# Both attention products that close a quad moved into one slot, the small one into the first projection's banks

## The chip, the core and the metric

The kernel runs on one core of one Trainium2 chip. A core has a matrix engine (TensorE, PE in the profile, with its weight loads shown apart as PEld), VectorE (DVE), ScalarE (ACT), GpSimd (POOL) and a queue that only issues transfers (SyncE, SP). Each engine works through its own list of instructions in order and waits on semaphores where it needs another engine's result. TensorE writes only to PSUM, which has eight banks of 128 x 512 float32. The metric is the device time of one execution in microseconds (us), smaller is better.

## The reference

Attention with a threshold, then a feed-forward layer with a hard-swish gate, on 8 batches of 8 heads, 576 tokens and a head size of 64:

```python
scores = scale * np.matmul(q, k.transpose(0, 1, 3, 2))
thresh = np.max(scores, axis=-1, keepdims=True) - tau
scores = np.where(scores >= thresh, scores, -1000000000.0)
attn = np.exp(scores - max); attn = attn / (sum + 1e-09)
x = matmul(attn, v)                 # heads side by side: 4608 tokens x 512
h = x @ w_in                        # 512 -> 2048
g = h * np.clip(h + 3.0, 0.0, 6.0) / 6.0
out = g @ w_out                     # 2048 -> 512
```

## The kernel before

**Tiling.** Two heads are a *pair*, two pairs a *quad*: 16 quads, two for each batch. A quad takes nine *slots*. Slots 0 to 3 hold the four blocks of 128 query rows of its first pair, slots 4 to 7 those of its second pair, and slot 8 the last 64 rows of all four heads. One flat loop runs over the 144 slots (its index is `n`), and the order in which this loop writes the instructions is the order in which every engine executes them; no scheduler rearranges them.

**One slot.** In the order of the loop body: ScalarE does the exponentials of the slot before (L290). VectorE takes the row maxima of this slot's scores and moves them from PSUM to SBUF (`sm_max`, L277), and GpSimd makes the bias (L280). If an item of the first projection is due (`todo1`, in all slots but 8), TensorE computes it (`mm1`, L353: eight matmuls into `h`, 256 or 320 tokens wide), ScalarE (slots 0, 1, 3, 5) or VectorE (slots 2, 4, 6, 7) makes relu(h + 3) (L362 or L364), and VectorE gates it into `g` (L370). VectorE takes the reciprocal of the sums (L293). Then come pieces of the second projection (`todo2`, `mm2_part`, L382: four matmuls each, four pieces to an output tile; after the fourth, L390 copies the tile out, and the next slot issues its transfer). One piece is done in a slot, none in slot 3, and once in a quad two in slot 0 or 1. ScalarE applies the mask (L285). Then comes one of the slot's own jobs: transposes of q and k for later slots (slots 1, 2, 5, 6, 7), or a product of the attention with v. At the end TensorE computes the scores of the *next* slot (L256, L262), and GpSimd normalises the slot before (L298), whose result SyncE transposes by DMA into `pT` or `pR`.

**The attention products.** `av_main` (L328) multiplies one pair's 512 rows with v: ten matmuls of 128x512 and a copy to `xT` (L335). It runs in slot 8 for the quad's first pair and in slot 3 of the next quad for its second pair. `av_rest` (L337) does the last 64 rows of both pairs: twenty matmuls of 64 columns and a copy (L343). It runs in slot 4 of the next quad. Each of the two functions issues its own copy right behind its matmuls.

**The banks.** The scores have two tiles of two banks. `h` is one tile of two banks, not doubled, so the matmuls of a projection item wait until the gate of the item before has read it. The output tile of the second projection has one bank (`o`), and one bank (`m`) serves, from index 28 on, all transposes and attention products in turn; before that `bank` alternates between the two. Together these are all eight banks.

**Supply of the projections.** The items of a batch are added in slot 4 of each even quad (16 items; a batch lasts two quads). The pieces of an output tile are added when the last item that it needs is taken, which happens in slot 4 of each quad from quad 3 on. In slot 4 the item is 256 wide in quads 3, 6, 7, 10, 11, 14 and 15 and 320 wide in the others. What is left at the end of the loop is done behind it.

Of the kernel before, what the change touches and what calls it, by code (L numbers as in the profile page):

```python
# [9 lines left out]
F32 = mybir.dt.float32  # L10
# [5 lines left out]
P = 128  # L16
# [5 lines left out]
def kernel(  # L22
# [10 lines left out]
    nc = tc.nc  # L33
# [28 lines left out]
    ps_h = ctx.enter_context(tc.psum_pool(name="ps_h", bufs=1))  # L62
# [5 lines left out]
    nat = {}  # L68
# [4 lines left out]
    xT = {}  # L73
# [42 lines left out]
    def load_v(b):  # L116
        vm = v_pool.tile([P, H, 4 * D], BF16, tag="vm", name="vm")
        vr = vrs[b % 2]
        vsb[b] = (vm, vr)
        for g in range(2):  # L120
            vcasts.append(lambda g=g: nc.gpsimd.dma_start(
                out=vm[:, g * 4:g * 4 + 4, :],
                in_=v[b, g * 4:g * 4 + 4, 0:512, :].rearrange("h (p t) d -> p h (t d)", t=4)))
        for a in range(2):
            vcasts.append(lambda a=a: nc.gpsimd.dma_start(
                out=vr[a * 64:(a + 1) * 64, a, :, :],
                in_=v[b, :, 512:S, :].rearrange("(hp a) p d -> a p hp d", a=2)[a]))
# [63 lines left out]
    def bank(name):  # L191
        nonlocal turn
        turn += 1
        if now < N2 and turn % 2:
            return ps_o.tile([P, 512], F32, tag="o", name=name)
        return ps_m.tile([P, 512], F32, tag="m", name=name)


    def copy_out(out, in_):
        if 0 <= now < N1:  # L200
            nc.vector.tensor_copy(out=out, in_=in_)
        else:
            nc.scalar.copy(out=out, in_=in_)  # L203


    def by_pe(pair):
        return pair // NPAIR < NB
# [16 lines left out]
    def transpose_k(pair):  # L224
        ps = main_pe(nat[pair // 2][1], pair)
        return lambda: copy_out(kT_of(pair)[:, 64:576], ps[:])

    def transpose_rest(quad):
        ps = bank("tr")
        nq, _, kr = nat[quad]  # L230
        nc.tensor.transpose(ps[:, 0:P], kr[:], identf[:])
        if by_pe(2 * quad):
            nc.tensor.transpose(ps[:, P:2 * P], nq[:, 1024:1152], identf[:])

        def evict():
            qT, kT = qkT[quad]
            both = ps[:].rearrange("p (w n t) -> p w n t", n=2, t=64)
            if by_pe(2 * quad):
                nc.vector.tensor_copy(out=qT[:, :, 512:S], in_=both[:, 1])
            copy_out(kT[0:64, :, S:S + 64], both[0:64, 0])  # L240
            copy_out(kT[64:P, :, 0:64], both[64:P, 0])
        return evict
# [49 lines left out]
    def sm_recip(sl):  # L292
        nc.vector.reciprocal(out=sl.rinv[:], in_=sl.rsum[:])  # L293
# [15 lines left out]
    def pe_transpose(sl):  # L309
        ps = ps_h.tile([P, 2, 1024], BF16, tag="h", name="pt")  # L310
        ps = ps[:].rearrange("p a b -> p (a b)")[:, 0:2 * S].rearrange("p (c t) -> p c t", t=P)
        pn = sl.pn[:].rearrange("p a b -> p (a b)")
        for c in range(9):
            nc.tensor.transpose(ps[:, c, :], pn[:, c * P:(c + 1) * P], identb[:])
        return lambda: nc.vector.tensor_copy(out=sl.dst, in_=ps)


    def av(ps, pair, pT, cols):
        b, hp = divmod(pair, NPAIR)
        vm, vr = vsb[b]  # L320
        for c in range(4):
            for a in range(2):
                nc.tensor.matmul(ps[a * 64:(a + 1) * 64, :], vm[:, 2 * hp + a, c * D:(c + 1) * D],  # L323
                                 pT[:, 5 * a + c, cols], start=(c == 0), stop=False)
        for a in range(2):
            nc.tensor.matmul(ps[a * 64:(a + 1) * 64, :], vr[:, a, hp, :], pT[:, 4, cols], start=False, stop=True)  # L326

    def av_main(pair):  # L328
        b, hp = divmod(pair, NPAIR)
        if hp == 0:  # L330
            xT[b] = x_pool.tile([P, KI, S], BF16, tag="xT", name="xT")
        ps = bank("av")
        av(ps[:], pair, pts[pair], slice(0, 512))
        o0 = 64 if b % 2 else 0
        nc.vector.tensor_copy(out=xT[b][:, hp, o0:o0 + 512], in_=ps[:])  # L335

    def av_rest(quad):  # L337
        b, g = divmod(quad, 2)
        ps = bank("ar")
        for n in range(2):  # L340
            av(ps[:, n * 64:(n + 1) * 64], 2 * quad + n, ptr[quad], slice(n * 64, (n + 1) * 64))
        o0 = 0 if b % 2 else 512
        nc.vector.tensor_copy(out=xT[b][:, 2 * g:2 * g + 2, o0:o0 + 64],  # L343
                              in_=ps[:, 0:P].rearrange("p (a b) -> p a b", a=2))

    def mm1(item, pool=None):
        b, ni, c0, w = item
        hps = (pool or ps_h).tile([P, 2, 512], F32, tag="s" if pool else "h", name="h")  # L350
        for n in range(2):
            for ki in range(KI):
                nc.tensor.matmul(hps[:, n, 0:w], w_in_sb[:, ki, (ni + n) * P:(ni + n + 1) * P],  # L353
                                 xT[b][:, ki, c0:c0 + w], start=(ki == 0), stop=(ki == KI - 1))
        return hps[:, :, 0:w]
# [61 lines left out]
    evict = transpose_k(0)  # L417
# [16 lines left out]
    for n, sl in enumerate(queue):  # L434
        quad, slot = sl.quad, sl.slot
        b, g = divmod(quad, 2)
        now = n
        if slot in (0, 4):
            pts[2 * quad + slot // 4] = pt_pool.tile([P, 9, 512], BF16, tag="pT", name="pT")
        if slot == 8:  # L440
            ptr[quad] = ptr_pool.tile([P, 9, P], BF16, tag="pR", name="pR")
        if quad == 0 and slot == 0:
            load_quad(1)
        if slot == (4 if quad else 8) and quad + 2 < NQUAD:
            load_quad(quad + 2)
        if slot == 0 and g == 1 and b + 1 < B:
            load_v(b + 1)
        if prev is not None:
            for i in range(2):
                sm_exp(prev, i)  # L450
        sm_max(sl)

        if slot != 8 and todo1:
            item, then = todo1.pop(0)
            h = mm1(item)
            r = mm1_relu(h, on_act=(slot in (0, 1, 3, 5)))
            mm1_gate(item, h, r)
            todo2.extend(then)
        copies = pe_transpose(queue[n - 2]) if n > 1 and queue[n - 2].on_chip else None
        if prev is not None:  # L460
            sm_recip(prev)
        if copies:
            copies()
        outs = []


        pieces = 0 if slot == 3 else 1
        if slot == 0:
            second = True
        if second and slot < 2 and len(todo2) > 1 and todo2[0][1] == todo2[1][1]:  # L470
            pieces, second = 2, False
        for _ in range(pieces):
            if todo2:
                bb, mt, part = todo2.pop(0)
                mm2_part(bb, mt, part)
                if part == 3:
                    outs += mm2_out(bb, mt, on_act=False)
        for i in range(2):
            sm_mask(sl, i)
        evict = None  # L480
        nxt = 2 * quad + 2
        if slot == (1 if quad else 2):
            evict = transpose_q(2 * quad + 1)
        elif slot == (2 if quad else 3):
            evict = transpose_k(2 * quad + 1)
        elif slot == 3 and quad > 0:
            av_main(2 * quad - 1)
        elif slot == 4 and quad > 0:
            av_rest(quad - 1)
            if quad % 2 == 0:  # L490
                todo1.extend(moe_of(quad // 2 - 1))
        elif slot in (5, 6, 7) and quad + 1 < NQUAD:
            if slot == 5:
                alloc_qk(quad + 1)
                evict = transpose_q(nxt)
            elif slot == 6:
                evict = transpose_k(nxt)
            else:
                evict = transpose_rest(quad + 1)
        elif slot == 8:  # L500
            av_main(2 * quad)
        if evict:
            evict()
        if n + 1 < len(queue):
            queue[n + 1].tiles = scores(queue[n + 1].quad, queue[n + 1].slot)
        if n < 8:
            warm_up(6)
        if prev is not None:
            sm_norm(prev)
        flush()  # L510
        late.extend(outs)
        start(loads, 1)
        if n < 4 or n > 12:
            start(vcasts, 1)
        if n > 3:
            start(casts, 1 if n < 24 else 2)
        prev = sl
# [7 lines left out]
    last = NQUAD - 1  # L525
# [16 lines left out]

    for item in todo1:
        rest1(*item)
    av_main(2 * last + 1)
    rest2()
    av_rest(last)
    for item in moe_of(B - 1):
        rest1(*item)
    rest2()  # L550
# [35 lines left out]
```

## Time and profile before

| | |
|---|---|
| median of 8 runs | 561.67 us (561.2 to 563.37) |
| the profiled execution: its time, its span | 561.59 us, 559.8 us |
| mean granted TensorE clock | 0.997 |
| first projection, L353 | 1024 matmuls |
| second projection, L382 | 576 matmuls |
| attention products, L323 `av` | 256 matmuls, 385 ns mean |
| row maxima, L277 | 288, 752 ns mean |
| gate, L370 | 128, 754 ns mean |
| copy of the large product, L335 | 32, 681 ns mean |
| copy of the small product, L343 | 16, 270 ns median |

A line of the page or the timeline gives the start in us (in a timeline), the busy time, the engine, the source line, the operation, output and inputs by the program's names, and the shape; `x8` means eight instructions merged into one line. What stands in brackets is the time that the engine stood idle just before, and whom it waited for. The ends of matmuls are modelled, so consecutive ones overlap in these lines, and the time from one start to the next is the safer measure. The idle time before a weight load (PEld) is not idle time of the matmuls.

### The profile page before, as it was taken

What the parts mean: (1) busy time and instruction counts of PE and PEld (TensorE: products, weight loads), DVE (VectorE), ACT (ScalarE), POOL (GpSimd) and SP (SyncE); (2) the same over time, 40 slices, a digit from 0 to 9 for tenths busy, and PEclk for the clock granted to TensorE, in tenths of its full rate; (3) what the DMA queues carried; (4) which work ended last, traced back from release to release, by engine and by line L of the source; (5) the groups of instructions that cost most, each with busy time, mean ns of one, the idle gap of its engine ahead of it and who ended that gap; (6) DMA issues with size and microseconds to landing.
All of it is one profiled execution on the core that took longest, in us unless ns stands there. A gap on an engine that the chain in (4) does not pass through costs nothing.

```text
span 559.8 us, 11634 instructions
## 1 busy us (share of the span) xinstructions
PE 533.5 (95%) x3856; PEld 309.8 (55%) x3856; DVE 424.3 (76%) x1040; ACT 469.9 (84%) x999; POOL 305.3 (55%) x646
## 2 busy tenths in 40 slices
PE   8898788899999999999999999999999999999997
PEld 6565455555555555655555565555555555654663
DVE  3687776787878788887978788887978788883540
ACT  3899989798889999899899999899888999983440
POOL 1878878854556555755556555754556555561000
PEclk9999999999999999999999999999999999999999
DMA  5889999996799878978699868977699866453102
GB/s 107 132 128 175 166 164 174 202 158 127 130 165 150 154 135 159 175 149 145 131 150 168 162 123 159 178 148 147 132 146 166 166 120 123 100 109 84 38 20 76
DMA packets 286204, 77.52 MB, mean 138 GB/s; under 512 B 269248, under 2 KB 281536, under 8 KB 286144
## 3 DMA queue, kind: packets, MB, share of 16 engines
q1 hardware_dynamic: 268736, 67.86, 65.0%
q0 software_dynamic: 17408, 8.92, 13.7%
q8 instruction: 30, 0.49, 0.4%
q14 instruction: 30, 0.25, 0.2%
HBM read 36.70 MB, written 9.44 MB: 82 GB/s over the span
## 4 chain that ended last, share of the span: by engine, by line
PE 58%; DVE 11%; ACT 7%; issue 3%; SPq 2%; DMA 2%; POOL 1%; DVEq 0%; POOLq 0%
PE o L382 17%; PE h L353 17%; PE s L256 15%; DVE s L277 5%; PE av L323 4%; ACT s L285 3%; ACT s L290 2%; DVE g L370 2%; DVE r L364 2%; ACT r L362 1%; PE tp L213 1%; DMA nq<-in_q_dram 1%; PE s L262 1%; DVE osb L390 1%; PE ar L323 1%
## 5 line engine op out<-in xcount | busy, mean ns | idle before, releaser
L298 POOL TENSOR_SCALAR pn<-s,rinv 128x576 bf16<-128x576 f32 x288 | 211.6, 745 | 133.9 <-DVE rinv L293 59.7
L277 DVE TENSOR_SCALAR_CACHE_REDUCE s<-s 128x576 f32<-128x576 f32 x288 | 205.8, 752 | 41.0 <-PE s L256 30.6
L285 ACT ACTIVATE s<-s,bias 128x576 f32<-128x576 f32 x288 | 207.0, 766 | 35.1 <-POOL bias L280 34.1
L290 ACT ACTIVATE s<-s 128x576 f32<-128x576 f32 x288 | 192.7, 671 | 0.3
L256 PE MATMUL s<-kT,qT 64*128 64x288 f32 x1024 | 170.8, 431 | 5.8 <-DVE s L277 3.2
L353 PE MATMUL h<-xT,w_in_sb 128*128 128x320 bf16 (+1 forms) x1024 | 145.6, 287 | 5.4 <-DVE g L370 4.3
L382 PE MATMUL o<-w_out_sb,g 128*128 128x512 bf16 x576 | 140.9, 379 | 3.6 <-DVE osb L390 3.0
L353 PEld LDWEIGHTS <-w_in_sb 128*128 128x128 bf16 x1024 | 92.3, 98 | 68.5 <-issue 30.2
L256 PEld LDWEIGHTS s<-kT,qT 64*128 64x128 f32 x1024 | 94.3, 186 | 62.2 <-DVE s L277 24.3
L370 DVE SCALAR_TENSOR_TENSOR g<-r,h 128x512 bf16<-128x512 f32 (+1 forms) x128 | 96.4, 754 | 41.4 <-ACT r L362 39.5
L280 POOL TENSOR_SCALAR bias<-m 128x1 f32<-128x1 f32 x288 | 54.4, 189 | 66.2 <-DVE s L277 46.2
L382 PEld LDWEIGHTS <-g 128*128 128x128 bf16 x576 | 55.6, 98 | 58.2 <-issue 9.8
L362 ACT ACTIVATE r<-h,three 128x640 f32<-128x640 f32 (+1 forms) x74 | 54.4, 736 | 20.6 <-PE h L353 19.9
L290 ACT ACTIVATION_READ_ACCUMULATOR s<-s 128x1 f32 x288 | 54.3, 188 | 0.0
L364 DVE TENSOR_SCALAR r<-h 128x512 f32<-128x512 f32 (+1 forms) x54 | 40.5, 751 | 0.0
L390 DVE TENSOR_SCALAR osb<-o 128x512 f32<-128x512 f32 x31 | 21.0, 676 | 22.2 <-PE o L382 22.2
L323 PE MATMUL av<-pT,vm 128*64 128x512 bf16 x256 | 33.7, 385 | 1.6 <-ACT kT L203 1.4
L293 DVE RECIPROCAL rinv<-rsum 128x2 f32<-128x2 f32 x144 | 23.0, 159 | 11.8 <-ACT s L290 11.0
L323 PEld LDWEIGHTS <-vm 128*64 128x64 bf16 x512 | 18.0, 110 | 24.3 <-issue 17.3
L335 DVE CAST xT<-av 128x512 bf16<-128x512 f32 x32 | 21.8, 681 | 5.4 <-PE av L326 5.1
L277 DVE DVE_READ_ACCUMULATOR s<-s 128x1 f32 x288 | 23.9, 83 | 0.0
L388 ACT ACTIVATE osb<-o 128x512 f32<-128x512 f32 x5 | 3.0, 597 | 23.9 <-PE o L382 23.9
(42 smaller groups left out, 257.2 us busy)
## 6 DMA issues: line engine op xcount, KB each, us to landing
km<-in_k_dram SPq DMA_DIRECT2D x64, 128.0 KB, 2.9
out_dram<-osb SPq DMA_DIRECT2D x32, 256.0 KB, 2.4
nq<-in_q_dram SPq DMA_DIRECT2D x96, 72.0 KB, 2.7
vm<-in_v_dram POOLq DMA_DIRECT2D x16, 256.0 KB, 5.5
nq<-in_q_dram SPq DMA_DIRECT2D x16, 128.0 KB, 4.6
w_in_sb<-in_moe_w_in_dram POOLq DMA_DIRECT2D x16, 128.0 KB, 4.4
w_out_sb<-in_moe_w_out_dram POOLq DMA_DIRECT2D x16, 128.0 KB, 5.0
pT<-pn SPq DMA_TRANSPOSE x119, 3.4
```

What stands on the lines that cost most here:

```text
L256: nc.tensor.matmul(tiles[a][:, hf, 0:HALF], qT_of(pair)[a * 64:(a + 1) * 64, t * P:(t + 1) * P], keys(pair, a, hf), start=True, stop=True)
L277: nc.vector.tensor_scalar(out=sl.s[:, i, :].rearrange("p (a b) -> p a b", a=2), in0=ps[:, :, 0:HALF], scalar1=1.0, scalar2=None, op0=Alu.m ...
L280: nc.gpsimd.tensor_scalar(out=sl.bias[:, i:i + 1], in0=sl.m[:, i:i + 1], scalar1=-scale, scalar2=tau, op0=Alu.mult, op1=Alu.add)
L285: nc.scalar.activation(out=s, in_=s, func=Act.Prelu, bias=sl.bias[:, i:i + 1], scale=scale, alpha=REJECT)
L290: nc.scalar.activation(out=s, in_=s, func=Act.Exp, accum_out=sl.rsum[:, i:i + 1])
L298: nc.gpsimd.tensor_scalar(out=pn[:, i, :], in0=sl.s[:, i, :], scalar1=sl.rinv[:, i:i + 1], scalar2=1.0, op0=Alu.mult, op1=Alu.mult)
L323: nc.tensor.matmul(ps[a * 64:(a + 1) * 64, :], vm[:, 2 * hp + a, c * D:(c + 1) * D], pT[:, 5 * a + c, cols], start=(c == 0), stop=False)
L353: nc.tensor.matmul(hps[:, n, 0:w], w_in_sb[:, ki, (ni + n) * P:(ni + n + 1) * P], xT[b][:, ki, c0:c0 + w], start=(ki == 0), stop=(ki == KI ...
L362: nc.scalar.activation(out=r, in_=hps, func=Act.Relu, bias=three[:])
L364: nc.vector.tensor_scalar(out=r, in0=hps, scalar1=3.0, scalar2=0.0, op0=Alu.add, op1=Alu.max)
L370: nc.vector.scalar_tensor_tensor(out=gbuf[:, ni:ni + 2, c0:c0 + w], in0=r, scalar=6.0, in1=hps, op0=Alu.min, op1=Alu.mult)
L382: nc.tensor.matmul(o_ps[0], gbuf[:, ni, mt * P:(mt + 1) * P], w_out_sb[:, ni, :], start=(ni == 0), stop=(ni == NI - 1))
```

## The change

From quad 3 on, slot 3 does no attention product and slot 4 does both, ahead of its item of the first projection. The small product goes no longer into the shared bank but into the last 128 columns of the second `h` bank, which a projection item (at most 320 columns) leaves free. Its copy is issued after the gate, the large product's copy between the item's matmuls and its relu. The slot without a piece of the second projection becomes slot 4 in place of slot 3. In earlier quads and behind the loop the order is as it was; `av_main` and `av_rest` now return their copies to be issued by the caller. Where the small product takes the `h` tile, it no longer calls `bank`.

```diff
     def av_main(pair):
...
-        nc.vector.tensor_copy(out=xT[b][:, hp, o0:o0 + 512], in_=ps[:])
-
-    def av_rest(quad):
+        return lambda: nc.vector.tensor_copy(out=xT[b][:, hp, o0:o0 + 512], in_=ps[:])
+
+    def av_rest(quad, ps=None):
         b, g = divmod(quad, 2)
-        ps = bank("ar")
+        ps = bank("ar") if ps is None else ps
...
-    def mm1(item, pool=None):
+    def mm1(item, pool=None, hps=None):
         b, ni, c0, w = item
-        hps = (pool or ps_h).tile([P, 2, 512], F32, tag="s" if pool else "h", name="h")
+        if hps is None:
+            hps = (pool or ps_h).tile([P, 2, 512], F32, tag="s" if pool else "h", name="h")
...
         sm_max(sl)
 
+        evicts = []
+        both = quad > 2 and slot == 4
+        hps = None
+        if both:
+            hps = ps_h.tile([P, 2, 512], F32, tag="h", name="h")
+            evicts.append(av_main(2 * quad - 1))
+            evicts.append(av_rest(quad - 1, hps[:, 1, 384:512]))
         if slot != 8 and todo1:
             item, then = todo1.pop(0)
-            h = mm1(item)
+            h = mm1(item, hps=hps)
+            if both:
+                evicts.pop(0)()
             r = mm1_relu(h, on_act=(slot in (0, 1, 3, 5)))
             mm1_gate(item, h, r)
             todo2.extend(then)
+        for evict in evicts:
+            evict()
...
-        pieces = 0 if slot == 3 else 1
+        pieces = 0 if slot == (4 if quad > 2 else 3) else 1
...
-        elif slot == 3 and quad > 0:
-            av_main(2 * quad - 1)
+        elif slot == 3 and 0 < quad < 3:
+            evict = av_main(2 * quad - 1)
         elif slot == 4 and quad > 0:
-            av_rest(quad - 1)
+            if not both:
+                evict = av_rest(quad - 1)
...
         elif slot == 8:
-            av_main(2 * quad)
+            evict = av_main(2 * quad)
...
-    av_main(2 * last + 1)
+    av_main(2 * last + 1)()
     rest2()
-    av_rest(last)
+    av_rest(last)()
```

More of the change, by code (lines that the diff above doesn't have):

```diff
@@ L228, in transpose_rest @@
     def transpose_rest(quad):
+        nq, _, kr = nat[quad]
         ps = bank("tr")
-        nq, _, kr = nat[quad]
         nc.tensor.transpose(ps[:, 0:P], kr[:], identf[:])
@@ L342, in av_rest @@
         o0 = 0 if b % 2 else 512
-        nc.vector.tensor_copy(out=xT[b][:, 2 * g:2 * g + 2, o0:o0 + 64],
-                              in_=ps[:, 0:P].rearrange("p (a b) -> p a b", a=2))
-    def mm1(item, pool=None):
+        return lambda: nc.vector.tensor_copy(out=xT[b][:, 2 * g:2 * g + 2, o0:o0 + 64],
+                                             in_=ps[:, 0:P].rearrange("p (a b) -> p a b", a=2))
+    def mm1(item, pool=None, hps=None):
         b, ni, c0, w = item
-        hps = (pool or ps_h).tile([P, 2, 512], F32, tag="s" if pool else "h", name="h")
+        if hps is None:
+            hps = (pool or ps_h).tile([P, 2, 512], F32, tag="s" if pool else "h", name="h")
         for n in range(2):
```

## The prediction

> **What bounds the kernel now.** I read the page's engine totals first, then the order of time on TensorE (PE) for one quad after another, then all engines side by side in slots 3 to 5. The totals:
>
> ```profile
> PE 533.5 (95%) x3856; PEld 309.8 (55%) x3856; DVE 424.3 (76%) x1040; ACT 469.9 (84%) x999; POOL 305.3 (55%) x646
> ```
>
> PE is the bound, but a busy PE includes matmuls stretched by a wait, so I took start-to-start times instead. In an undisturbed slot the next piece starts after a fixed time: scores 1.17 us, first projection 0.88 (256 wide) or 1.10 (320 wide), 0.98 or 1.19 where the next piece has 64-wide weights, one second-projection piece 0.86 to 0.95, the large product 1.20, the small one 0.44. What a slot takes beyond that is lost. From 106 us (slot 4 of quad 3) to the end of the queue near 502 us the losses over 0.08 us add up to 10.5 us. Thus no rearrangement of these slots can win more than about 10.5. The largest losses look like this (PE, in order of time):
>
> ```profile
> 122.53 1.02 PE L382 MATMUL o<-w_out_sb,g 128*128 128x512 bf16 x4 [0.55 <-DVE osb L390]
> ...
> 134.95 1.91 PE L256 MATMUL s<-kT,qT 64*128 64x288 f32 x8
> 137.22 1.26 PE L353 MATMUL h<-xT,w_in_sb 128*128 128x320 bf16 x8 [0.36 <-DVE g L370]
> ```
>
> At 134.95 the scores need 2.27 to the next start instead of 1.17: PE waits for the gate, because the h banks are single. At 122.53 the output bank is still being copied out. Now slots 4 and 5 of a quad with 256-wide items (all engines, in order of time):
>
> ```profile
> 204.45 1.05 PE L353 MATMUL h<-xT,w_in_sb 128*128 128x256 bf16 x8
> ...
> 205.34 1.03 PE L382 MATMUL o<-w_out_sb,g 128*128 128x512 bf16 x4
> ...
> 206.00 0.69 DVE L364 TENSOR_SCALAR r<-h 128x512 f32<-128x512 f32 x1
> ...
> 206.73 0.69 DVE L370 SCALAR_TENSOR_TENSOR g<-r,h 128x512 bf16<-128x512 f32 x1
> 206.73 0.79 PEld L256 LDWEIGHTS s<-kT,qT 64*128 64x128 f32 x8
> 206.73 1.24 PE L256 MATMUL s<-kT,qT 64*128 64x288 f32 x8
> ...
> 207.41 0.27 DVE L343 CAST xT<-ar 128x128 bf16<-128x128 f32 x1
> ...
> 207.90 0.77 PEld L353 LDWEIGHTS <-w_in_sb 128*128 128x128 bf16 x8 [0.39 <-DVE xT L343]
> 207.90 1.05 PE L353 MATMUL h<-xT,w_in_sb 128*128 128x256 bf16 x8
> ```
>
> After slot 4's projection (204.45) PE has a second-projection piece, the small product and the scores, 3.45 us in all, before slot 5's projection (207.90) needs the same banks. VectorE's relu, gate and small eviction hide under that.
>
> **The change, part by part.** It holds in quads 3 to 15, 13 quads; the built order of instructions confirms it. PE's work is the same: the large product goes from after slot 3's projection to before slot 4's, the small one with it, and one second-projection piece from slot 4 to slot 3. The sum of the start-to-start times is unchanged.
>
> *The new wait.* After slot 4's projection PE now has only slot 5's scores; then slot 5's projection waits until the h banks are free. Count from the start s of slot 4's projection. 256 wide: it ends at s+1.05, relu starts 0.04 later, the gate 0.72 after the relu, the small eviction 0.60 after the gate, it takes 0.27, and a projection starts about 0.05 after its releaser: s+2.73. PE is ready at s+0.98+1.17 = s+2.15, so it stands 0.58. 320 wide: 1.26+0.04+0.85+0.74+0.27+0.05 = 3.21 against 1.19+1.17 = 2.36, so 0.85. Slot 4's item is 256 wide in quads 3, 6, 7, 10, 11, 14, 15 and 320 wide in 4, 5, 8, 9, 12, 13: 7 x 0.58 + 6 x 0.85 = 9.2. Queued on VectorE ahead of the relu is now the large eviction: scores 1.24 + 0.13 + row maxima 1.44 + copy 0.67, done before the projection ends, except in quads 9 and 13, where an output copy (0.67) moves into slot 3 and a late gate delays it: 0.34 and 0.76 more. New loss: 10.3. Behind the small eviction wait the reciprocal (1.2 later), then POOL's normalisation (1.47) and slot 5's bias; ScalarE has slot 5's relu to do until then, so I cost that at nothing; without that cover it would be up to 0.5 a quad.
>
> *The other new wait.* The small product waits for slot 3's gate (same banks). In the quad above that gate ends at 203.92; the product would come about 205.3. Latest in quad 13: gate end 425.19 against 425.5. Cost nothing; mm1 and scores would queue behind it. Its transposed operand is issued 9 us earlier and lands in 3.2 to 8.8 us (median 4.8); moving it up by about 0.8 leaves it covered.
>
> *What comes back.* All second-projection pieces run one slot later, so the output copies move too. (a) The losses at 122.53 and its kind, copies of slot 7 that stop slot 8's piece (0.61, 0.64, 0.58, 0.59, 0.93), go: -3.35; three quads (6, 10, 14) get one at about 0.6: +1.8. (b) Slot 2 of quads 4 and 5, the loss at 134.95 (1.25 each), gets a piece as cover; slot 3 then has none and its scores wait for the row maxima, about 0.47: net -1.6. (c) Quads 7 and 11 lose 0.33 + 0.63 where an output copy and the q transpose meet in slot 5; the copy leaves: -1.9. Quads 8 and 12 get that meeting, about 0.45 each: +0.9. (d) Waits for slot 3's gate at slot 4's projection (0.51, 0.27, 0.17, 0.12, 0.12), one of 0.35 behind slot 5 of quad 3, and 0.2 each in quads 8 and 12 for the small eviction: -1.9. Sum: -6.1. Each output copy takes its DMA issue (about 0.55 on SP) one slot later, past at most one 1.3 us transpose issue; transposed rows are read four or more slots later, so nothing.
>
> *Not shown before.* Scores straight into the large product occurs once (1.26, against 1.13 into a second-projection piece), scores into a projection at 1.17: between 0 and 0.1 a quad, up to +1.2. I take 0, as the same weight width change between projection and product is already in the 0.98. The give-back may lie between nothing but (a), about -1.5, and the whole 10.5.
>
> Sum: 10.3 - 6.1 = +4.2 on the profiled execution's 561.59 (span 559.8): 565.8. The median of the runs, 561.67, stands 0.1 above it, within what single runs differ.
>
> *The clock.* A wait can cost clock too. The trace has one such place:
>
> ```profile
> 92.22:95.56 3.34, 1.91 (x8) 1.06 (x9) 2.07 (x7) 3.31 (x8) 2.45 (x6) 1.00 1.29 153
> 95.56:99.76 4.20, 4.20 (x20) 2.88 (x20) 2.71 (x8) 2.80 (x7) 3.66 (x8) 0.59 1.28 224
> 103.85:107.93 4.08, 2.50 (x20) 1.43 (x19) 1.03 (x5) 4.08 (x10) 3.35 (x7) 1.00 1.46 185
> ```
>
> The columns are stretch, length, busy time of PE, PEld, DVE, ACT, POOL, granted clock, DMA. After 1.43 idle in 3.34 the clock fell to 0.59 and the next pieces cost 1.6 more; after 1.58 idle in 4.08 it held. The new wait leaves PE 0.6 to 0.85 idle in about 3.5, less than both, so I take no loss; at worst 1.6 in each quad, 21 us.
>
> The Trainium skill, "TensorE: Matmul & The Clock Gate", What's actually happening, says the clock halves after at least one idle window of about 3.4 us. By that rule the new wait could never cost clock, and the sum would stay as it is; the row at 92.22, where PE was busy for over half the stretch and the clock still fell, speaks against leaning on it.
>
> **The rivals.**
> 1. The new wait appears and the give-back fails: the copies that move meet other work. For it: VectorE's slots 5 already carry the q transpose (0.77) and copies (0.67). With only (a) returned, and the 1.2 above: +8.8 to +10, 570.4 to 571.6.
> 2. Everything lost today is absorbed by the new wait, which gives VectorE and ScalarE time: 10.3 - 10.5 = -0.2, 561.4. Against it: (a) returns in quads 6, 10 and 14 by construction.
> 3. Faster: relu, gate and eviction finish under the scores, so the new wait is small. It decides from 0.4 a quad (5.2 in all): below that, 5.2 - 6.1 is a gain; at 0.2 it is 2.6 - 6.1 = -3.5, 558.1. For it: PE gets 1.64 of work ahead of slot 4's projection. Against: relu and gate alone, 1.3 us, exceed the 1.17 of scores, and the banks are single.
> 4. Clock drops: up to 21 more, 570 to 587.
> 5. The change does nothing: excluded, the order of instructions on PE and VectorE differs.
>
> **How the numbers follow.** The forecast has 0.64 (own range 563 to 569), rival 1 0.19, rival 2 0.09, rival 3 0.05, rival 4 0.03. Leaving out the clock case and most of the gain, the range is 561.0 to 572.0. Within 0.2% (1.1 us, about what this kernel's runs can tell from no change) lie rival 2 and little of the forecast's low end: 0.10; faster 0.05; slower 0.85.
>
> **What would show it.** Slot 5's projection in quads 3 to 15 starts with an idle of 0.5 to 0.9 before it, released by the small eviction; scores before it last as now. Waits of slot 8's pieces for output copies remain only in quads 6, 10, 14. The granted clock stays at 1.00. I am wrong if that idle is missing or below 0.4, if the clock shows drops after 110 us, or if the total of losses outside slot 5 does not shrink from 10.5 towards 4.4.

## The result and the profile after

The changed kernel takes 565.32 us in the median (564.32 to 568.78, 12 runs); beside it the kernel before took 561.95 (561.0 to 565.77). The ratio is 1.0061, with a 95% interval of 1.0045 to 1.0077: the change costs 0.6%, 3.4 us between the medians. The profiled execution took 565.47 us, span 563.7, at a mean granted clock of 0.990 (before: 561.59, 559.8, 0.997).

The totals of the page and the groups of the two projections, of the changed kernel. After the bar stand the busy time, the mean ns of one, and the idle time just before, with its releaser:

```profile
PE 533.4 (95%) x3856; PEld 310.0 (55%) x3856; DVE 424.3 (75%) x1040; ACT 470.4 (83%) x999; POOL 305.3 (54%) x646
...
L354 PE MATMUL h<-xT,w_in_sb 128*128 128x320 bf16 (+1 forms) x1024 | 145.6, 288 | 11.8 <-DVE xT L343 8.8
L383 PE MATMUL o<-w_out_sb,g 128*128 128x512 bf16 x576 | 140.7, 379 | 2.2 <-DVE osb L391 1.6
```

The same two groups of the kernel before:

```profile
L353 PE MATMUL h<-xT,w_in_sb 128*128 128x320 bf16 (+1 forms) x1024 | 145.6, 287 | 5.4 <-DVE g L370 4.3
L382 PE MATMUL o<-w_out_sb,g 128*128 128x512 bf16 x576 | 140.9, 379 | 3.6 <-DVE osb L390 3.0
```

PE's work is what it was. What has changed is the idle time at the first projection: 11.8 us now, of which 8.8 end with line 343, the copy of the small product. Before, it was 5.4 us, most of it ended by the gate, and no wait for that copy was among them. At the second projection 2.2 us of idle are left of 3.6: fewer pieces stand behind an output copy. The place of the new wait, in quad 6, all engines in order of time:

```profile
204.50 1.05 PE L354 MATMUL h<-xT,w_in_sb 128*128 128x256 bf16 x8
...
205.48 1.24 PE L256 MATMUL s<-kT,qT 64*128 64x288 f32 x8
205.58 0.69 DVE L365 TENSOR_SCALAR r<-h 128x512 f32<-128x512 f32 x1 [0.36 <-PE h L354]
...
206.31 0.69 DVE L371 SCALAR_TENSOR_TENSOR g<-r,h 128x512 bf16<-128x512 f32 x1
...
206.91 0.28 DVE L343 CAST xT<-h 128x128 bf16<-128x128 f32 x1
...
207.26 1.05 PE L354 MATMUL h<-xT,w_in_sb 128*128 128x256 bf16 x8 [0.54 <-DVE xT L343]
```

From projection to projection the chain takes 2.76 us (207.26 - 204.50): the projection itself, then relu, gate and small copy one after the other. PE has 0.98 + 1.17 = 2.15 to do meanwhile and stands for the rest, 0.61. A 320-wide item, and the place that lost 1.25 before (slot 2 of quad 4), in one stretch of PE:

```profile
138.02 1.82 PE L256 MATMUL s<-kT,qT 64*128 64x288 f32 x8
139.77 1.05 PE L323 MATMUL av<-pT,vm 128*64 128x512 bf16 x8
...
142.47 1.24 PE L256 MATMUL s<-kT,qT 64*128 64x288 f32 x8
144.52 1.26 PE L354 MATMUL h<-xT,w_in_sb 128*128 128x320 bf16 x8 [0.80 <-DVE xT L343]
```

The scores at 142.47 need 2.05 to the next start instead of 1.17: 0.88 lost. At 138.02, slot 3, they need 1.75 into the large product: 0.58, where slot 2 had lost 1.25. What became of the wait for an output copy in slot 8, here in quad 6:

```profile
217.40 1.02 PE L383 MATMUL o<-w_out_sb,g 128*128 128x512 bf16 x4 [0.53 <-DVE osb L391]
```

By start-to-start times, slot 5 loses 0.61 in each of seven quads and 0.87 to 0.88 in each of six, 9.5 us in all. Everything else from 106 us to the end of the queue loses 4.9 us instead of 10.5; 0.9 of the 4.9 is in quad 3, where the large product runs at half clock (shown below), and 4.0 is the rest.

One stretch of PE can be compared without the clock: the eleven quads from the scores of slot 8 of quad 4 to those of quad 15. In none of the profiles does the clock fall there. The kernel before takes 345.21 us for them (153.50 to 498.71), the changed kernel 347.55 (153.57 to 501.12), and two further profiles of the changed kernel and one of the kernel before, taken for the experiments, repeat this to 0.05. The experiments are compared by this stretch too.

### The profile page after: what moved, and what is told of

Read it like the earlier page. It is cut to its first block, busy times and chain, and to the rows that moved or that the text cites. A ratio compares the mean times of both kernels' runs of the same rounds, so it can differ in the third digit from the quotient of the medians.

```text
span 563.7 us, 11642 instructions
## 1 busy us (share of the span) xinstructions
PE 533.4 (95%) x3856; PEld 310.0 (55%) x3856; DVE 424.3 (75%) x1040; ACT 470.4 (83%) x999; POOL 305.3 (54%) x646
## 5 line engine op out<-in xcount | busy, mean ns | idle before, releaser
L354 PE MATMUL h<-xT,w_in_sb 128*128 128x320 bf16 (+1 forms) x1024 | 145.6, 288 | 11.8 <-DVE xT L343 8.8
```

## The experiments

In these, theory A is the prediction's: slot 5's projection stands because only the scores cover the chain of relu, gate and small copy, and each microsecond of cover or of chain counts in full. B: VectorE's queue is the limit, and the wait only shows at that place. C: the price is half clock in quad 3. D: only the place of the second-projection piece costs. E: the spread of those pieces is the whole gain of the fastest version. F: in quad 3 the small product waits for the landing of its operand, and that is part of the price.

**The small product left where it was.** The large product is moved, and the slot without a piece is slot 4, as in the changed kernel; the small product stays at the end of slot 4, in the shared bank, so the banks of the first projection are free of it.

```diff
         if both:
-            hps = ps_h.tile([P, 2, 512], F32, tag="h", name="h")
             evicts.append(av_main(2 * quad - 1))
-            evicts.append(av_rest(quad - 1, hps[:, 1, 384:512]))
...
-            if not both:
-                evict = av_rest(quad - 1)
+            evict = av_rest(quad - 1)
```

> One part alone: the large product moves ahead of slot 4's projection and the piece of the second projection to slot 3, but the small product stays at the end of slot 4 in the shared bank, its copy last. Theory A (slot 5's projection stands because only the scores, 1.17 us, cover relu, gate and small copy; every microsecond of cover pays in full): PE has 0.44 more ahead of slot 5's scores and the h banks are free 0.27 sooner, so the wait falls from 0.61 and 0.88 to 0 (256 wide) and about 0.2 (320 wide), 1.2 us over six quads instead of 9.5: about 557 to 559, clearly faster than the kernel before. Rival B (VectorE's queue with the large copy in slot 4 is the limit, the wait at slot 5 is only where it shows): the wait moves to the next scores or gate, 564 to 566. Rival C (the halved clock in quad 3 is the main price): stays near 565, since quad 3's slot 3 is as in the changed kernel.

Measured: 561.75 us, 0.9974 of before (0.9955 to 0.9992), thus slightly faster than before. PE of this kernel in quad 6:

```profile
203.66 0.32 PE L323 MATMUL ar<-pR,vm 128*64 128x64 bf16 x8
...
204.09 1.24 PE L256 MATMUL s<-kT,qT 64*128 64x288 f32 x8
205.27 0.94 PE L354 MATMUL h<-xT,w_in_sb 128*128 128x256 bf16 x7
```

Slot 5's projection follows the scores by 1.18, without idle; where the item is 320 wide it still loses about 0.2 in four of six quads. So the wait comes with the small product's move, which does two things at once: it puts a copy at the end of the chain and takes the product away as cover. This run doesn't tell the two apart. Moving the large product and the piece without it is a small gain. B, which kept the loss, and C fall. The gain against the changed kernel is 0.87%, 4.9 us, less than A expected. In the eleven quads it is 3.9 (343.65 against 347.55). Waits of 8.1 go there, but the small product now waits for its bank (1.7 in all, 0.4 each in quads 5 and 13), the 320-wide items of quads 8, 9 and 12 keep 0.7, later projections wait 0.4, and the cheaper succession of pieces (below, 1.2) goes; 0.2 stays open.

**A longer chain.** The small product's copy is issued twice; everything else stays.

```diff
         for evict in evicts:
             evict()
+            evict()
```

> The changed kernel with the small product's copy issued twice in quads 3 to 15 (0.27 us more on VectorE, same result). Theory A: the copy stands in the chain that frees the h banks, so slot 5's projection waits 0.88 and 1.15 instead of 0.61 and 0.88, 13 x 0.27 = 3.5 us: about 568.8. Rival B (the wait is a symptom of VectorE's load over the whole quad): VectorE has 24% idle, the 0.27 vanishes in it, 565 to 566. Rival C (clock): no change, 565.3.

Measured: 570.47 us, 1.0128 (1.0107 to 1.0149), 0.67% or 3.8 us above the changed kernel. All engines of this kernel in quad 6:

```profile
207.72 1.24 PE L256 MATMUL s<-kT,qT 64*128 64x288 f32 x8
...
208.56 0.69 DVE L371 SCALAR_TENSOR_TENSOR g<-r,h 128x512 bf16<-128x512 f32 x1
...
209.16 0.61 DVE L343 CAST xT<-h 128x128 bf16<-128x128 f32 x2
...
209.83 0.94 PE L354 MATMUL h<-xT,w_in_sb 128*128 128x256 bf16 x7 [0.86 <-DVE xT L343]
```

The copies take 0.61 instead of 0.28, and the projection comes 2.11 after the scores instead of 1.78. 13 times 0.33 is 4.3; 3.8 reached the end. In the eleven quads the kernel takes 351.09, 3.54 more than the changed one, 0.32 a quad. The chain stands in the path that sets the end, microsecond for microsecond, as A says; B's 565 to 566 and C's 565.3 are missed.

**The piece back in slot 4.** One second-projection piece covers slot 5's chain again, and slot 3 has none, as before the change.

```diff
-        pieces = 0 if slot == (4 if quad > 2 else 3) else 1
+        pieces = 0 if slot == 3 else 1
```

> The changed kernel, but the slot without a piece of the second projection is slot 3 again, and slot 4 has one between its projection and slot 5's scores. Theory A: slot 5's wait goes (3.0 us of work against 2.73 needed, 320 wide 3.22 against 3.21), -9.5; but slot 3 has nothing between its projection and slot 4's scores, which then wait for the row maxima, 0.6 (320) to 0.8 (256) in each of 13 quads, +9, and the output copies are back where they were before, +4: about 569, slower than the changed kernel. Rival B: 565. Rival D (only the piece's place costs, slot 3 needs no cover because ScalarE and VectorE catch up): 556 to 558.

Measured: 565.28 us, 1.0047 (1.0031 to 1.0062). PE of this kernel in quad 6:

```profile
202.12 1.82 PE L256 MATMUL s<-kT,qT 64*128 64x288 f32 x8
203.87 1.05 PE L323 MATMUL av<-pT,vm 128*64 128x512 bf16 x8
...
207.23 1.24 PE L256 MATMUL s<-kT,qT 64*128 64x288 f32 x8
208.41 1.05 PE L354 MATMUL h<-xT,w_in_sb 128*128 128x256 bf16 x8
```

Slot 5's wait is gone (208.41 follows 207.23 by 1.18), and slot 3 has it instead: its scores need 1.75 to the next start, 0.58 lost. This hole of 0.50 to 0.58 stands in ten of the thirteen quads (0.22 in quads 4 and 5, none in quad 3), and the waits for output copies in slot 8 are back. So the place of the piece only chooses which slot stands: D, which expected a gain, falls. A's 569, slower than the changed kernel, was wrong too: it made the hole too large, and the kernel is no slower (1.0047 against 1.0061, overlapping intervals; 348.07 against 347.55 in the eleven quads). The number fits B, which the two runs above speak against.

**One piece in every slot.** Two second-projection pieces are no longer run together early in a batch, and no slot goes without.

```diff
-        pieces = 0 if slot == (4 if quad > 2 else 3) else 1
+        pieces = 1
...
-        if second and slot < 2 and len(todo2) > 1 and todo2[0][1] == todo2[1][1]:
+        if False and second and slot < 2 and len(todo2) > 1 and todo2[0][1] == todo2[1][1]:
```

> The changed kernel with one piece of the second projection in every slot, 3 and 4 too, and no double piece in slot 0 or 1, so nine pieces a quad as before. Theory A: the wait at slot 5 goes (-9.5); slots 0 and 1 have one piece less to cover slot 0's gate, as slots 1 and 5 have today, which cost 0 to 0.3 there: +0 to 4; output copies land elsewhere, +-1.5. About 556 to 561, faster than before. Rival B: the wait reappears in slots 0 to 2, where ScalarE makes the relu, 564 to 567.

Measured: 559.97 us, 0.9939 (0.9917 to 0.9962). PE of this kernel in quad 6:

```profile
206.69 1.05 PE L354 MATMUL h<-xT,w_in_sb 128*128 128x256 bf16 x8
207.57 1.03 PE L383 MATMUL o<-w_out_sb,g 128*128 128x512 bf16 x3
208.53 1.24 PE L256 MATMUL s<-kT,qT 64*128 64x288 f32 x8
209.70 1.05 PE L354 MATMUL h<-xT,w_in_sb 128*128 128x256 bf16 x8
```

The next projection comes 3.01 us after the last, more than the chain's 2.76: the wait is covered with 0.25 to spare. It isn't in quads 9 and 13, where slot 5 still stands for the small copy and loses 0.39 and 0.74. In quad 13, all engines:

```profile
424.57 0.82 DVE L371 SCALAR_TENSOR_TENSOR g<-r,h 128x640 bf16<-128x640 f32 x1 [1.87 <-ACT r L363]
...
425.89 1.26 PE L354 MATMUL h<-xT,w_in_sb 128*128 128x320 bf16 x8
...
427.93 0.81 DVE L365 TENSOR_SCALAR r<-h 128x640 f32<-128x640 f32 x1
...
429.85 1.05 PE L354 MATMUL h<-xT,w_in_sb 128*128 128x256 bf16 x8 [0.67 <-DVE xT L343]
```

Slot 3's gate (424.57) comes late behind ScalarE's relu, and slot 4's relu (427.93) starts 0.78 after its projection ended (425.89 + 1.26).

**The same spread in the kernel before.** The same two edits, without the change.

> The kernel before with one piece of the second projection in every slot and none doubled, the products where they were (large in slot 3, small in slot 4). It tells whether the gain of the kernel with a piece in each slot (0.9939) comes from the pieces alone. Theory A: slot 5 was covered before anyway, so only the output copies and the cover of slots 0 and 1 change; the cheaper order of the products next to each other (about 1.6 us) and the covered wait for slot 3's gate (about 1.2) are missing: 560 to 563, ratio 0.997 to 1.002. Rival E (the spread of the pieces is the whole gain and moving the products gives nothing): ratio 0.993 to 0.995.

Measured: 559.67 us, 0.9934 (0.9913 to 0.9955), the same within the intervals as with the change. PE of this kernel in quad 6, where slots 3, 4 and 5 each have their piece:

```profile
201.02 1.24 PE L256 MATMUL s<-kT,qT 64*128 64x288 f32 x8
202.20 1.05 PE L353 MATMUL h<-xT,w_in_sb 128*128 128x256 bf16 x8
203.08 1.03 PE L382 MATMUL o<-w_out_sb,g 128*128 128x512 bf16 x4
...
204.47 1.24 PE L256 MATMUL s<-kT,qT 64*128 64x288 f32 x8
205.65 1.05 PE L353 MATMUL h<-xT,w_in_sb 128*128 128x256 bf16 x8
```

E is right and A's expectation for this kernel wrong: the gain of 0.6% is the spread's. With a piece in every slot, moving the products neither gives nor costs anything that the medians show; in the eleven quads the version with the change takes 343.31, the one without 343.96. These two versions beat both kernels.

**Quad 3: idle work ahead of the scores.** Six transposes in slot 0 and ten in slot 3 of quad 3, whose results nobody reads, keep PE busy where the clock had been lost.

```diff
+        if quad == 3 and slot in (0, 3):
+            fill = ps_o.tile([P, 512], F32, tag="o", name="fill")
+            for _ in range(6 if slot == 0 else 10):
+                nc.tensor.transpose(fill[:, 0:P], identf[:], identf[:])
```

> The changed kernel with 6 and 10 idle transposes of 128x128 put on PE in front of the scores that slots 0 and 3 of quad 3 issue, where PE stood 0.8 and 1.5 us in its profile; their results are used by nobody. Theory C (the half clock at 105 to 108 us in the profile of the changed kernel is a price of the change, because the hole in slot 3 lost the large product as cover, and it comes in most executions): with PE busy there the drop goes, 1.6 us faster, ratio to before about 1.003, and the granted clock of quad 3 is 1.00. Theory A with its own account (the drops come and go from execution to execution, as in those of the kernel before, and the medians of both kernels carry about as many): 0 to 0.8 us faster, ratio 1.005 to 1.006.

Measured: 566.38 us, 1.0056 (1.0032 to 1.0080), as the changed kernel. The clock was 1.00 from 96 to 112 us in its profile, and still the small product waits, here in order of time on PE:

```profile
105.22 1.24 PE L256 MATMUL s<-kT,qT 64*128 64x288 f32 x8 [0.95 <-ACT kT L203]
106.39 1.05 PE L323 MATMUL av<-pT,vm 128*64 128x512 bf16 x8
107.28 0.38 PE L326 MATMUL av<-pT,vr 128*64 128x512 bf16 x2
109.07 0.32 PE L323 MATMUL h<-pR,vm 128*64 128x64 bf16 x8 [1.41 <-DMA pR<-pn]
```

With the clock held in quad 3, this execution is no faster, and neither is the median. What sets the start at 109.07 here is the landing of the small product's transposed operand, issued at 100.4, 8.6 us earlier. C falls above all by the eleven quads: +2.3 of the difference arises where the clock is full.

In the changed kernel the small product starts at 109.12, but for another reason. On PE:

```profile
107.09 1.92 PE L323 MATMUL av<-pT,vm 128*64 128x512 bf16 x8
...
109.12 0.29 PE L323 MATMUL h<-pR,vm 128*64 128x64 bf16 x8
```

The issue of its operand, and the time until that had landed:

```profile
L306 SPq DMA_TRANSPOSE pR<-pn x1: 3097/3097/3097, 99.6 to 99.6; - x1
...
DMA to landing us min/median/max: 7.6/7.6/7.6
```

The operand had landed at 107.2 and PE did not stand: the large product, at half clock until 109.01, lasted until the small one started. The expectation of the next run takes this for a wait for the landing, which it isn't.

**The change from quad 4 on.** If a wait for the landing is part of the price, leaving quad 3 as it was must win it back.

```diff
-        both = quad > 2 and slot == 4
+        both = quad > 3 and slot == 4
...
-        elif slot == 3 and 0 < quad < 3:
+        elif slot == 3 and 0 < quad < 4:
```

> The changed kernel, but in quad 3 the two products stay where the kernel before has them (large at the end of slot 3, small at the end of slot 4, in the shared bank); the pieces of the second projection are as in the changed kernel everywhere. It prices a wait that the profiles of the changed kernel and of the one with idle transposes show in quad 3 alone: the small product, moved up by about 2 us there, stands until its transposed operand has landed (8.6 us after its issue, at about 109.05). Theory F (that wait costs about 1.4 us, and slot 5's wait in quad 3 another 0.6): 1.5 to 2.2 us faster than the changed kernel, ratio to before 1.0020 to 1.0035 where the changed kernel has 1.006. Rival (the landing only takes the place of the wait for the first key copy and for slot 3's gate, which the kernel before has there too, 0.27): 0 to 0.5 us faster.

Beside it the changed kernel as it is:

> The changed kernel itself, timed beside the kernel with quad 3 left alone, on the same chip. All theories: ratio to before 1.005 to 1.007.

Measured: 565.78 us, 1.0058 (1.0038 to 1.0078), and 565.51 us, 1.0057 (1.0039 to 1.0075). F falls as a price: its 1.0020 to 1.0035 is missed, and none of the three profiles of the changed kernel shows that wait. In quad 3 PE stands longest for the first key copy, in this version ahead of the large product:

```profile
107.14 1.92 PE L323 MATMUL av<-pT,vm 128*64 128x512 bf16 x8 [2.04 <-ACT kT L203]
```

The changed kernel timed beside it stands 2.03 for the same copy, ahead of the scores. So quad 3 has its largest hole in either order.

**Both kernels once more**, to see whether the drop of the clock in quad 3 belongs to the change.

> The changed kernel once more, one look. Theory C: its profile has the half clock in slots 3 and 4 of quad 3 again, near 105 to 108 us. Theory A: the place of the drops, or their number, differs from the profile seen (two, at 96 and 105 us); slot 5's waits are 0.61 and 0.88 again, to 0.02.

> The kernel before once more, one look. Theory C: one drop, at 96 us, as in the profile seen. Theory A: drops elsewhere or in another number are as likely, none of them after 112 us, where PE no longer stands for more than a microsecond in any stretch.

Measured, one run each: 566.33 and 562.49 us, spans 564.6 and 560.7. The columns of these stretches are length, busy time (and instructions) of PE, PEld, DVE, ACT and POOL, granted clock, DMA share and GB/s. First the changed kernel in the first profile:

```profile
104.00:108.00 4.00, 2.79 (x14) 1.36 (x16) 0.90 (x3) 4.00 (x10) 3.12 (x7) 0.70 1.42 205
108.00:112.00 4.00, 3.75 (x44) 2.25 (x40) 3.24 (x8) 3.32 (x8) 2.45 (x5) 0.87 1.46 166
```

The changed kernel again:

```profile
104.00:108.00 4.00, 3.20 (x14) 1.68 (x16) 1.30 (x3) 4.00 (x10) 3.00 (x7) 0.53 1.47 177
```

The changed kernel timed beside the version from quad 4 on:

```profile
104.00:108.00 4.00, 1.97 (x17) 1.17 (x18) 0.57 (x3) 3.92 (x9) 3.66 (x9) 1.00 1.46 207
```

The kernel before, again:

```profile
104.00:108.00 4.00, 1.94 (x17) 1.24 (x18) 0.57 (x3) 3.87 (x9) 3.66 (x9) 1.00 1.46 194
```

The same stretch of the same kernel is run at 0.70, 0.53 and 1.00. The second profile alone would have met C's expectation; the third does not, and the kernel before, again, has its one drop at 60.4 us instead of 96. The drop is not a constant part of the change's price.

## Why the prediction was right

It said 565.8 us, slower, 4.2 more than before; measured was 565.32, 3.4 more between the medians and 3.9 between the profiled executions. Point by point:

- *The new wait.* 0.58 and 0.85 were forecast, 0.61 and 0.87 to 0.88 measured: 9.5 us against 9.2. The prediction's sum from the kernel before's own durations held to 0.03 us a quad, and the longer chain, the returned piece and the small product left in place show the uncovered chain to be the cause.
- *Quads 9 and 13* were to lose 0.34 and 0.76 more. They lose nothing more: this term was wrong by 1.1. In quad 13 the gate ends at 426.26, output copy and large copy follow, and the relu starts at 428.92, just as the projection ends at 428.88. The step assumed the late gate of before and overlooked that the double piece of these two quads moves from slot 0 to slot 1. With one piece in every slot, thus none doubled, the gate is late again and 0.39 and 0.74 are lost, nearly the sizes forecast; the double piece alone was not tested.
- *What comes back*: forecast from 10.5 down to 4.4, measured 4.0, and 4.9 with quad 3's half clock. (a) 0.60, 0.59 and 0.60 stand in quads 6, 10, 14 (0.6 forecast); (b) 0.58 in slot 3 of quads 4 and 5 (0.47); (c) 0.39 and 0.40 in quads 8 and 12 (0.45). Rival 1 (nothing but (a) returns) and rival 2 (all of it is absorbed) are refuted by these rows.
- *"Cost nothing" for the small product's own wait* held from quad 4 on. In quad 3 of the changed kernel's three profiles PE stands 0, 0 and 0.20 for it, the last for slot 3's gate, and never for the operand's landing. "Leaves it covered" held there by 0.6 to 1.9: with the idle transposes in front, the product waited 1.41 for the landing.
- *"The sum of the start-to-start times is unchanged"*, with 0 to 1.2 more for orders not shown before, had the wrong sign. Measured: large into small product 1.10 (into the scores 1.20), small product into projection 0.41 (into the scores 0.44), scores into large product 1.17. It is about 0.1 less a quad. Over the eleven quads the difference is 347.55 - 345.21 = +2.34, of which waits make +3.5 and the order -1.2.
- *The end*, not in the forecast: behind the loop PE waits 1.13 for a gate where it waited 0.65, +0.5. And as all pieces run one slot later, one of them, about 0.9, is done behind the loop that was done ahead of slot 8 of quad 4: PE has 44 instead of 48 matmuls of the second projection up to there and 140 instead of 136 behind slot 8 of quad 15. That shifts time and adds none.
- *The clock.* No drop starts after 110 us before the last matmul, as forecast, so the new waits of 0.6 to 0.9 cost none and rival 4 falls. But the clock did not stay at 1.00: the profiled execution has three drops up to 109 us, and quad 3, which the new order reaches first, had no term for it. Rival 3 falls with the size of the wait, 0.61 where it needed less than 0.4.

In the profiled executions: +0.1 up to slot 8 of quad 4, +2.3 in the eleven quads, +1.5 behind, 3.9 in all. With the displaced piece counted where it was before, these are +1.0 (quad 3's clock is in it), +2.3 and +0.6. The forecast +4.2 has its two largest terms right; the 1.1 of quads 9 and 13 and the 1.2 of the order, both too dear, are met by quad 3 and the end, which it left out. That the total is nearer than its parts is luck.

## What to carry to other kernels

Where a bank is single, ask what TensorE has to do between the writer's end and the reader's last copy: that much other work must stand behind the writer, and work moved ahead of the writer no longer counts. Moving a filler from one slot to another moves the hole; spreading the fillers one to a slot closed it here in eleven of thirteen quads, and both orders of the products then took the same time within the intervals (0.9939 and 0.9934). A new reader queued at the end of such a chain costs its own length in each round: 0.28 us became 0.61, and 3.8 us reached the end over 13 rounds.

## What the runs showed of the hardware

The granted clock differs between executions of one kernel: the changed kernel's spans are 562.5, 562.6 and 563.1 at a mean clock of 0.999 and 567.0 at 0.988; the kernel before's lie at 559.2 to 559.9 at 0.999 and above, and at 563.8 and 564.1 at 0.988. At full clock the change thus costs about 3.0 us, and part of the spread of single runs goes with the clock. Apart from one in each execution behind its last matmul, all drops in the profiles begin by 107.1 us and end by 113.9, where PE has the largest holes. A stretch with PE busy for 1.94 or 1.97 of 4.00 us kept the full clock in some executions, and in others it fell at the same place; what decides was not found. One thing shows, here in the first profile of the changed kernel:

```profile
54.40:57.81 3.41, 3.39 (x17) 2.36 (x17) 1.48 (x5) 2.80 (x7) 3.15 (x7) 0.50 1.46 143
95.36:98.77 3.41, 3.29 (x16) 2.36 (x16) 2.15 (x8) 2.69 (x7) 3.01 (x5) 0.50 1.27 207
105.60:109.01 3.41, 3.41 (x18) 1.51 (x16) 1.91 (x5) 3.41 (x9) 2.41 (x7) 0.50 1.35 222
```

The drops last 3.41 us (in other executions also 6.83), and their starts lie 12 and 3 times 3.41 apart. Whether a hole costs clock may hang on how it falls into this raster; that was not tested.

The transposed operand of the small product in quad 3 took 6.6, 7.6 and 8.5 us from issue to landing in the three profiles of the changed kernel, 7.8 and 8.8 in the two of the kernel before, where the median of all quads is 4.8. A lead that looks ample by the median is used up there: with 8.6 in the run with idle transposes, PE stood 1.41.
